# Weight loads on the scalar engine's queue, and a plan that counts transferred bytes, in an attention and channel-mix kernel

## The chip, the cores and the metric

The kernel runs on one core of one Trainium2 chip. The metric is the device time of one execution in microseconds (us), median of three runs. The engines are called by their profile names: PE (matrix products), DVE (VectorE), ACT (ScalarE), POOL (GpSimd) and SP (SyncE, which computes nothing and here issues transfers). Each engine works through its own queue strictly in the order in which the program lists its instructions.

## The reference

Inputs: q, k, v of shape 8 x 8 x 1152 x 64 (batch, heads, tokens, head size) in float32, and the weights of a channel mix, `w_k` 512 x 1024, `w_v` 1024 x 512 and `w_r` 512 x 512. Cut to what matters, the reference computes

```python
q_pool = q.reshape(B, H, S // 2, 2, D).mean(axis=3)          # 576 queries per head
scores = (q_pool @ k.T) / sqrt(D)
attn   = exp(scores - max); attn /= sum(attn) + 1e-9
out    = attn @ v                                            # then heads side by side: x, 8 x 576 x 512
x_prev = x shifted by one token
k = relu((mu_k * x + (1 - mu_k) * x_prev) @ w_k)
r = sigmoid((mu_r * x + (1 - mu_r) * x_prev) @ w_r)
result = r * ((k * k) @ w_v)
```

## The kernel before

**Attention.** A head is loaded by `prep` (keys `kr`, values `vr`, 288 KB each, split there into a coarse and a fine half-precision part `kn`, `vt`, `vb`) and every second head `queries` loads the queries `qr` of two heads in two pieces. Transposing transfers issued by SP (L432, L407) turn `kn` into `ks1` and the queries `qn` into `qT`; L435 copies `ks1` into a second tile `ks2`, which the second pass of scores reads (the trace calls both `ks`). A head has six blocks of 96 queries (`block`), 384 blocks in all. For each block PE makes scores (L473) in one of three buffers `s`, DVE takes the maximum over the keys (`mx`, L480, then `mb`, L486), PE spreads it (L483, L488), ACT writes it beside the fine part of the queries (L491), PE adds the fine part of the scores (L497), ACT exponentiates into `pf` (L503), POOL splits off the low bits `pl` (L505), and `window` multiplies by the values (L523, L525, L530).

**Channel mix.** When the eight heads of a batch element are done, `ff` runs its products (L663) over tiles of 256 tokens. In the first batch element there is no such work yet.

**Weights.** `weights` loads the three matrices in twenty pieces of 512 KB, eight of `w_k`, four of `w_r`, eight of `w_v`, each into one of two staging buffers `st` (L581). A piece is converted by ACT (L592, into the one PSUM bank `f`), three DVE instructions (L594, L595, L597), ACT (L599) and POOL (L600). A buffer of `st` is free again when the L597 of its piece has ended. All twenty conversions lie in the first batch element.

**Order.** No instruction is issued where it is written. The calls of `op` (`Issue.add`) collect 'operations' with an engine, an assumed duration, the buffers read and written, and a key. `Issue.run` then simulates list scheduling under two sets of paddings (`PLANS`), improves the order for eight rounds, judges each order on three trials with randomly lengthened durations and waits, and issues the best one. Each engine's order is thereafter fixed. A transfer is an operation on a planned engine "DMA" (SP's queue): an assumed issue time, then a fixed `tail` until its data are there (2.0 to 4.5 us), whatever else is being transferred; in the trials up to `LATE_DMA` = 1.5 us are added to it. Some buffers are named as read by the first two weight loads only so that the plan puts these loads after them.

**Completion.** Transfers signal through eight semaphores that are used in rotation in the order of the program, and a transfer first waits until the one eight before it has landed.

Of the kernel before, what the change touches and what calls it, by code (L numbers as in the profile page):

```python
# [20 lines left out]
P = 128  # L21
# [20 lines left out]
PER, PACE = 2.75, 2.4  # L42
# [5 lines left out]


PLANS = ((0.08, 0.1), (0.12, 0.15))  # L50
LATE, SLACK, LATE_DMA = 0.06, 0.06, 1.5

class Issue:
# [17 lines left out]
                return self.LAT[k]  # L73
        return 0.18

    def add(self, eng, dur, fn, r=(), w=(), key=0.0, port=None, tail=2.0):
        n = len(self.ops)
        deps = {}

        def dep(m, war):  # L80
            e = self.ops[m][0]
            lat = self.ops[m][6] if e == "DMA" else 0.0 if war and e == eng else self.lat(e, eng)
            deps[m] = max(deps.get(m, 0.0), lat)

# [12 lines left out]
        for b in r:
            if b not in w:
                self.rd.setdefault(b, []).append(n)
        self.ops.append((eng, dur, fn, key, deps, eng == "POOL" if port is None else port, tail))  # L100

    @staticmethod
    def play(eng, dur, pred, succ, prio, wait, port):
# [155 lines left out]
def kernel(  # L259
# [12 lines left out]
    nc = tc.nc  # L272
    B, H, S, D = q.shape
# [16 lines left out]
    const = ctx.enter_context(tc.tile_pool(name="const", bufs=1))  # L290
    psum = ctx.enter_context(tc.tile_pool(name="psum", bufs=1, space=PSUM))
    iss = Issue()
    op = iss.add

    def bufs(name, n, shape, dt):
        return [const.tile(shape, dt, name=f"{name}{i}") for i in range(n)]
# [81 lines left out]
    def queries(n, key):  # L378
# [4 lines left out]
        JS = ((0, 5), (5, NQ))  # L383
        for j0, j1 in JS:
            js = slice(j0, j1)
            op("DMA", 0.36, lambda js=js: nc.sync.dma_start(qr[0][:, js], qv[:, js]), w=[("qr", j0)],
               key=key - 2 * NB * PER, tail=3.0)
            op("DVE", (j1 - j0) * D / 960 + 0.069, lambda js=js: nc.vector.tensor_tensor(
                qs[0][:, js], qr[0][:, js, 0:D], qr[0][:, js, D:2 * D], op=ALU.add),
               r=[("qr", j0)], w=[("qs", j0)], key=key, port=True)  # L390
            op("ACT", (j1 - j0) * P / 1200 + 0.093, lambda js=js, j1=j1, j0=j0: nc.scalar.activation(
                qn[0][:, 0, js].rearrange("p j (r d) -> p j r d", r=2),
                qs[0][:, js].unsqueeze(2).broadcast_to([P, j1 - j0, 2, D]), AF.Copy, scale=SQ),
               r=[("qs", j0)], w=[("qn", j0)], key=key + 1)
            op("DVE", (j1 - j0) * D / 960 + 0.069, lambda js=js: nc.vector.scalar_tensor_tensor(
                qn[0][:, 1, js, 0:D], qs[0][:, js], SQ, qn[0][:, 0, js, 0:D], op0=ALU.mult, op1=ALU.subtract),
               r=[("qs", j0), ("qn", j0)], w=[("qnl", j0)], key=key + 2, port=True)
            if n and j0 == 0:
                continue

            g0 = 0 if n else j0
            gs = slice(g0, j1)
            blocks = [(hh, jj, g) for g, g1 in JS for hh in (0, 1) for jj in range(NB)
                      if g0 <= g < j1 and hh * TQ + jj * QN < g1 * P and hh * TQ + (jj + 1) * QN > g * P]
            js_ = [g for g, _ in JS if g0 <= g < j1]
            for r_, m, t_ in ((0, "qn", "qT"), (1, "qnl", "qTl")):
                op("DMA", 1.25, lambda gs=gs, r_=r_: nc.sync.dma_start_transpose(  # L407
                    qT[i][:, r_, gs], qn[0][:, r_, gs].rearrange("p j x -> p (j x)")),
                   r=[(m, g) for g in js_] + ([("qn", g) for g in js_] if r_ else []),
                   w=[(t_, i) + b_ for b_ in blocks], key=key + 2, tail=2.0)  # L410

    def prep(n, key):

        b, h = divmod(n, H)
        i, j = n % 2, n % NV
        def dma(o, src, buf):
            op("DMA", 0.36, lambda: nc.sync.dma_start(o, src), w=[buf], key=key - 2 * NB * PER, tail=2.8)

        dma(kr[i], k[b, h].rearrange("(p c) d -> p c d", c=NC), ("kr", i))
        dma(vr[i], v[b, h].rearrange("(p c) d -> p c d", c=NC), ("vr", i))  # L420
        for c0, c1 in ((0, 5), (5, NC)):
# [7 lines left out]
               lambda cs=cs, en=nc.vector if ve else nc.gpsimd: en.tensor_tensor(  # L429
                   kn[i][:, cs, D:P], kr[i][:, cs], kn[i][:, cs, 0:D], op=ALU.subtract),  # L430
               r=[("kr", i), ("kn", i, c0)], w=[("knl", i, c0)], key=key + 1, port=True)
        op("DMA", 1.3, lambda: nc.sync.dma_start_transpose(ks1[i], kn[i].rearrange("p c x -> p (c x)")),  # L432
           r=[(m, i, c0) for m in ("kn", "knl") for c0 in (0, 5)], w=[("ks1", i, 0), ("ks1", i, 5)],
           key=key + 1, tail=2.0)
        op("DMA", 0.47, lambda: nc.sync.dma_start(ks2[i][0:D], ks1[i][0:D]),  # L435
           r=[("ks1", i, 0), ("ks1", i, 5)], w=[("ks2", i)], key=key + 1, tail=2.5)
        for c0, c1 in ((0, 5), (5, NC)):
            cs = slice(c0, c1)
            nn = (c1 - c0) * D
# [128 lines left out]
    def weights(n, w, kc, key, step):  # L568
        cols = w.shape[1]
        wv = w.bitcast(I32).rearrange("(c p) (f t) -> c p f t", p=P, t=2)  # L570
        for c in range(kc):
            for f in range(0, cols, 512):
# [8 lines left out]
                op("DMA", 0.36, lambda s3=s3, src=wv[c, :, f:f + 512]: nc.sync.dma_start(s3, src),  # L581
                   r=[("ks1", 1, 0), ("ks2", 0), ("vr", 1)] if iss.nw <= 2 else [], w=[ks], key=key, tail=4.5)
# [64 lines left out]
    def ff(t0, t1, key, tail):  # L647
# [49 lines left out]
        for s0 in range(0, n, P):  # L697
# [24 lines left out]
            for f in range(NF):  # L722
# [4 lines left out]
            op("DVE", 0.605, lambda e=e, m_=m_, ps=ps[:, 0:DM]: nc.vector.scalar_tensor_tensor(  # L727
                m_, ps, 0.5 / (SV * SV * SW), e, op0=ALU.mult, op1=ALU.mult),
               r=[pk, ke], w=[km], key=key + O_DONE)
            op("DMA", 0.36, lambda m_=m_, t=t0 + s0: nc.sync.dma_start(out_f[t:t + P], m_), r=[km], key=key)  # L730
        return key


# [65 lines left out]
```

## Time and profile before

| what | value |
|---|---|
| median of 3 runs | 1170.27 us (1168.08 to 1170.37) |
| the profiled execution's own time | 1168.73 us |
| its span, first to last instruction | 1166.8 us |
| mean granted clock of PE | 0.995 |
| first product of PE | 11.99 us |
| first and last conversion of a weight piece (start of L592) | 27.9 and 147.0 us |

The profile is of one execution, and times in it count from the first instruction. 'Busy' of an engine is the time in which at least one of its instructions ran; the idle time before an instruction is put down to what ended it last. Rows of SP are the times that its queue took to issue a transfer; when the data are there is given apart, as 'to landing'.

### The profile page before, as it was taken

How to read it: one execution, taken by the hardware profiler on the slowest of the kernel's cores; microseconds unless marked ns; L12 is line 12 of the kernel's file. 1: busy time of each engine (PE TensorE's matmuls, PEld its weight loads, DVE VectorE, ACT ScalarE, POOL GpSimd, SP SyncE). 2: the span in 40 equal slices, each digit the busy share in tenths (PEclk: the TensorE clock that was granted, in tenths of full speed). 3: DMA queues.
4: the chain of work that ended last, by engine and by line, in shares of the span. 5: the costliest groups of instructions: out<-in, count | busy, mean ns of one | idle time of the engine just before them, and what ended most of it. 6: DMA issues, size and time to landing. Idle time of an engine off the chain costs nothing.

```text
span 1166.8 us, 45860 instructions
## 1 busy us (share of the span) xinstructions
PE 1116.0 (96%) x19504; PEld 928.6 (80%) x19504; DVE 834.0 (71%) x1558; ACT 858.8 (74%) x1746; POOL 713.1 (61%) x819
## 2 busy tenths in 40 slices
PE   3878899999999999999999999999999999999998
PEld 3767787988788887978788888979797988888565
DVE  6899987777777867777676867776677877673320
ACT  4878887887877787777777686868777778765643
POOL 3777776656666575746666575756665666543431
PEclk9899999999999999999999999999999999999999
DMA  9696845566455534555344535444544344310000
GB/s 223 180 240 171 188 101 129 120 142 113 88 116 117 136 68 103 123 113 123 87 113 114 105 89 119 113 102 108 113 114 107 93 102 93 72 27 12 19 19 28
DMA packets 222380, 126.69 MB, mean 109 GB/s; under 512 B 157664, under 2 KB 194528, under 8 KB 222176
## 3 DMA queue, kind: packets, MB, share of 16 engines
q1 hardware_dynamic: 222176, 123.77, 47.1%
q8 instruction: 152, 2.49, 0.9%
q14 instruction: 52, 0.43, 0.1%
HBM read 67.11 MB, written 9.44 MB: 66 GB/s over the span
## 4 chain that ended last, share of the span: by engine, by line
PE 84%; ACT 5%; DVE 5%; DMA 3%; issue 2%; SPq 0%; ACTq 0%; DVEq 0%
PE f L663 33%; PE s L497 11%; PE s L473 11%; PE a L530 7%; PE a L523 6%; PE a L525 6%; PE s L663 4%; ACT pf L503 2%; DVE mx L480 2%; PE s L483 2%; PE a L663 2%; PE s L488 1%; PE a L560 1%; DMA qT<-qn 1%; DMA st<-in_moe_w_r_dram 1%
## 5 line engine op out<-in xcount | busy, mean ns | idle before, releaser
L505 POOL TENSOR_SCALAR pl<-pf 128x864 f16<-128x864 uint16 x384 | 365.8, 953 | 252.0 <-ACT pf L503 221.2
L480 DVE TENSOR_REDUCE mx<-s 128x96 f16<-128x864 f32 x384 | 402.3, 1054 | 139.1 <-PE s L473 82.1
L503 ACT ACTIVATE pf<-s 128x864 int32<-128x864 f32 x384 | 338.6, 891 | 87.9 <-PE s L497 66.8
L473 PE MATMUL s<-qT,ks 128*128 128x96 f16 x3456 | 217.9, 207 | 23.6 <-DMA qT<-qn 12.0
L525 PE MATMUL a<-vt,pf 128*128 128x64 f16 x2880 | 237.6, 193 | 0.0
L523 PE MATMUL a<-vt,pf 128*128 128x65 f16 x2880 | 237.2, 193 | 0.2
L497 PE MATMUL s<-qT,ks 128*128 128x96 f16 x3456 | 216.0, 207 | 9.7 <-ACT qT L491 8.8
L473 PEld LDWEIGHTS <-ks 128*128 128x128 f16 x3456 | 183.2, 99 | 45.1 <-issue 18.2
L523 PEld LDWEIGHTS <-pf 128*128 128x128 f16 x2880 | 202.3, 98 | 5.6
L497 PEld LDWEIGHTS <-ks 128*128 128x128 f16 x3456 | 181.2, 98 | 31.2 <-issue 12.1
L525 PEld LDWEIGHTS <-pf 128*128 128x128 f16 x2880 | 193.1, 98 | 7.4 <-issue 0.4
L491 ACT ACTIVATE qT<-s 1x96 f16<-1x96 f32 x384 | 92.9, 243 | 111.2 <-PE s L488 97.5
L486 DVE TENSOR_REDUCE mb<-s 96x1 f16<-96x128 f32 x384 | 109.0, 285 | 82.0 <-PE s L483 72.4
L530 PE MATMUL a<-vb,pl 128*128 128x65 f16 x2880 | 152.7, 194 | 1.0 <-POOL pl L505 0.9
L663 PE MATMUL f<-xhk,wk_hi 128*128 128x256 f16 x496 | 135.1, 272 | 0.4 <-ACT r L690 0.4
L663 PE MATMUL f<-xhk,wk_lo 128*128 128x256 f16 x496 | 135.1, 272 | 0.0
L663 PE MATMUL f<-xlk,wk_hi 128*128 128x256 f16 x496 | 135.1, 272 | 0.0
L530 PEld LDWEIGHTS <-pl 128*128 128x128 f16 x2880 | 121.4, 98 | 6.3 <-POOL pl L505 1.6
L663 PEld LDWEIGHTS <-wk_hi 128*128 128x128 f16 x1152 | 106.2, 98 | 10.9 <-issue 0.6
L429 POOL TENSOR_TENSOR kn<-kr,kn 128x320 f16<-128x320 f32 x126 | 99.7, 802 | 20.5 <-ACT kn L424 16.1
L694 POOL TENSOR_TENSOR gl<-g 128x512 f16<-128x512 f32 x72 | 77.8, 1080 | 50.0 <-ACT g L692 47.8
L663 PE MATMUL f<-wv_hi,g 128*128 128x512 f16 x240 | 90.9, 379 | 0.9 <-ACT em L713 0.6
(93 smaller groups left out, 1989.9 us busy)
## 6 DMA issues: line engine op xcount, KB each, us to landing
kr<-in_k_dram SPq DMA_DIRECT2D x64, 288.0 KB, 3.0
vr<-in_v_dram SPq DMA_DIRECT2D x64, 288.0 KB, 3.0
qr<-in_q_dram SPq DMA_DIRECT2D x32, 320.0 KB, 3.5
ks<-ks SPq DMA_DIRECT2D x64, 144.0 KB, 2.6
out_dram<-em SPq DMA_DIRECT2D x36, 256.0 KB, 2.1
qr<-in_q_dram SPq DMA_DIRECT2D x32, 256.0 KB, 3.5
st<-in_moe_w_k_dram SPq DMA_DIRECT2D x8, 512.0 KB, 4.5
st<-in_moe_w_v_dram SPq DMA_DIRECT2D x8, 512.0 KB, 4.0
```

What stands on the lines that cost most here:

```text
L429: lambda cs=cs, en=nc.vector if ve else nc.gpsimd: en.tensor_tensor(kn[i][:, cs, D:P], kr[i][:, cs], kn[i][:, cs, 0:D], op=ALU.subtract),
L473: nc.tensor.matmul(cols(c, c + 1), ks1[hp][:, c, :], qhi, start=(c == c0), stop=False, skip_group_check=True)
L480: op("DVE", 0.967, lambda: nc.vector.tensor_reduce(mxz, grid(0, NC).rearrange("p c q -> p q c"), axis=AX.X, op=ALU.max), r=[("s", z)], w=[ ...
L486: op("DVE", 0.199, lambda: nc.vector.tensor_reduce(mbz[0:QN], s[0:QN, 0:P], axis=AX.X, op=ALU.max), r=[("s", z)], w=[("mb", z)], key=t + O ...
L491: op("ACT", 0.133, lambda: nc.scalar.activation(qlo[QN:QN + 1], s[QN:QN + 1, 0:QN], AF.Prelu, scale=1.0 - EPS, alpha=(1.0 + EPS) / (1.0 - ...
L497: nc.tensor.matmul(cols(c, c + 1), ks2[hp][:, c, :], qlo, start=False, stop=True, skip_group_check=True)
L503: op("ACT", NC * QN / 1200 + 0.051, lambda: nc.scalar.activation(pf[:, :, rows], grid(0, NC), AF.Exp, bias=SHIFT, scale=0.125 / (2.0 * SQ) ...
L505: op("POOL", NC * QN / 1000 + 0.066, lambda: nc.gpsimd.tensor_scalar(pl[:, :, rows], half(pf, U16, 0)[:, :, rows], LO, 1.0, op0=ALU.mult, ...
L523: nc.tensor.matmul(a_b[:, a0:a0 + VN], half(pf, F16, 1)[:, c, rows], vt[jv][:, c, D:D + VN], start=(w == 0 and c == 0), stop=False, skip_g ...
L525: nc.tensor.matmul(a_b[:, a0:a0 + D], half(pf, F16, 1)[:, c, rows], vt[jv][:, c, 0:D], start=False, stop=False, skip_group_check=True)
L530: nc.tensor.matmul(a_b[:, a0:a0 + VN], pl[:, c, rows], vb[jv][:, c, 0:VN], start=False, stop=(c == NC - 1), skip_group_check=True)
L663: nc.tensor.matmul(ps, terms[i][0], terms[i][1], start=(first and i == 0), stop=(i == last), skip_group_check=True)
```

## The change

It has four parts.

- A new method `move` enters a transfer as two planned operations: its issue on the engine that issues it, and, `lead` = 1.0 us later, its bytes on a planned resource "BYTES" that serves one transfer at a time at 215 KB per us, with 0.4 us until the data count as there. All transfers but the two small ones of `mu_k` and `mu_r` use it. "BYTES" issues nothing; it exists in the plan alone.
- The twenty weight loads are issued by ACT (`nc.scalar.dma_start`), with an assumed issue time of 0.40 us, and their key is lower by two steps of the sequence of pieces.
- `LATE_DMA` is 0.8 in place of 1.5.
- The fixed tails go, since `move` replaces them.

```diff
-LATE, SLACK, LATE_DMA = 0.06, 0.06, 1.5
+LATE, SLACK, LATE_DMA = 0.06, 0.06, 0.8
...
-            lat = self.ops[m][6] if e == "DMA" else 0.0 if war and e == eng else self.lat(e, eng)
+            lat = self.ops[m][6] if self.ops[m][6] else 0.0 if war and e == eng else self.lat(e, eng)
...
+    def move(self, kb, eng, dur, fn, r=(), w=(), key=0.0, lead=1.0, tail=0.4):
+
+        self.add(eng, dur, fn, r=r, w=w, key=key, tail=lead)
+        self.add("BYTES", kb / 215.0, lambda: None, r=r, w=w, key=key, tail=tail)
...
-            op("DMA", 0.36, lambda: nc.sync.dma_start(o, src), w=[buf], key=key - 2 * NB * PER, tail=2.8)
+            move(288, "DMA", 0.4, lambda: nc.sync.dma_start(o, src), w=[buf], key=key - 2 * NB * PER)
...
-        op("DMA", 0.47, lambda: nc.sync.dma_start(ks2[i][0:D], ks1[i][0:D]),
-           r=[("ks1", i, 0), ("ks1", i, 5)], w=[("ks2", i)], key=key + 1, tail=2.5)
+        move(200, "DMA", 0.47, lambda: nc.sync.dma_start(ks2[i][0:D], ks1[i][0:D]),
+           r=[("ks1", i, 0), ("ks1", i, 5)], w=[("ks2", i)], key=key + 1)
...
-                op("DMA", 0.36, lambda s3=s3, src=wv[c, :, f:f + 512]: nc.sync.dma_start(s3, src),
-                   r=[("ks1", 1, 0), ("ks2", 0), ("vr", 1)] if iss.nw <= 2 else [], w=[ks], key=key, tail=4.5)
+
+                move(512, "ACT", 0.40, lambda s3=s3, src=wv[c, :, f:f + 512]: nc.scalar.dma_start(s3, src),
+                   r=[("ks1", 1, 0), ("ks2", 0), ("vr", 1)] if iss.nw <= 2 else [], w=[ks], key=key - 2.0 * step)
```

The same instructions with the same operands are issued as before, apart from the queue of the twenty loads. But the plan is made anew, so the order changes on every engine. In the new file the lines lie 6 or 7 further down: L581 is L588, L592 is L599, L597 is L604, L480 is L486, L486 is L492, L491 is L497, L503 is L509, L407 is L413, L417 is L423, L432 is L438, L435 is L441. Numbers behind a name tell its buffers apart (`ks_0_79` and `ks_1_80` are the two `ks1`, `ks_0_81` and `ks_1_82` the two `ks2`; `st_121` and `st_120` the two staging buffers).

Three places matter below. The first is the start: SP's queue behind the first eight loads (keys, values, queries and the two `mu`). Before:

```order
L432 DMA_TRANSPOSE ks_0_79<-kn_76 128x9x128
L386 DMA qr_74<-in_q_dram 128x5x128
L407 DMA_TRANSPOSE qT_83<-qn_78 128x5x128
L386 DMA qr_74<-in_q_dram 128x4x128
L435 DMA ks_0_81<-ks_0_79 64x1152
```

Now:

```order
L392 DMA qr_74<-in_q_dram 128x5x128
L413 DMA_TRANSPOSE qT_83<-qn_78 128x5x128 x2
L438 DMA_TRANSPOSE ks_0_79<-kn_76 128x9x128
L438 DMA_TRANSPOSE ks_1_80<-kn_77 128x9x128
L392 DMA qr_74<-in_q_dram 128x4x128
L413 DMA_TRANSPOSE qT_83<-qn_78 128x4x128 x2
L441 DMA ks_0_81<-ks_0_79 64x1152
```

The first queries are turned ahead of the first keys, and the copy into the first `ks2` has moved behind four further transposing transfers.

The second is where the weight loads begin. SP's queue before (a few us after the rows above):

```order
L417 DMA kr_70<-in_k_dram 128x576
L407 DMA_TRANSPOSE qT_83<-qn_78 128x4x128
L581 DMA st_121<-in_moe_w_k_dram 128x1024
L581 DMA st_120<-in_moe_w_k_dram 128x1024
L435 DMA ks_1_82<-ks_1_80 64x1152
L417 DMA vr_72<-in_v_dram 128x576
L386 DMA qr_74<-in_q_dram 128x5x128
L386 DMA qr_74<-in_q_dram 128x4x128
```

ACT's queue before, behind the second exponential (`kr_70` and `vr_72` hold the third head's keys and values here):

```order
L491 ACTIVATE qT_83<-s_130 1x96
L391 ACTIVATE qn_78<-qs_75 128x512
L424 CAST kn_76<-kr_70 128x5x64
L424 CAST kn_76<-kr_70 128x4x64
L503 ACTIVATE pf<-s_130 128x9x96
L440 ACTIVATE vt_87<-vr_72 128x5x64
L592 ACTIVATE f<-st_121 128x512
L491 ACTIVATE qT_83<-s_128 1x96
```

ACT's queue now, from the first block's L491 (now L497) to the first conversion:

```order
L497 ACTIVATE qT_83<-s_128 1x96
L588 DMA st_121<-in_moe_w_k_dram 128x1024
L588 DMA st_120<-in_moe_w_k_dram 128x1024
L497 ACTIVATE qT_83<-s_129 1x96
L509 ACTIVATE pf<-s_128 128x9x96
L397 ACTIVATE qn_78<-qs_75 128x512
L509 ACTIVATE pf<-s_129 128x9x96
L497 ACTIVATE qT_83<-s_130 1x96
L430 CAST kn_76<-kr_70 128x5x64
L430 CAST kn_76<-kr_70 128x4x64
L509 ACTIVATE pf<-s_130 128x9x96
L599 ACTIVATE f<-st_121 128x512
```

The two loads have left SP's queue, and `vt_87`, which reads the third head's values, no longer stands ahead of the first conversion; it comes five rows after the last one shown, behind the fifth exponential.

The third is the end of the conversions, in DVE's queue. Before, the twentieth stands ahead of the maximum of the 57th block:

```order
L595 SCALAR_TENSOR_TENSOR f<-st_120,f 128x512
L486 TENSOR_REDUCE mb_97<-s_129 96x1
L597 SCALAR_TENSOR_TENSOR ex_116<-st_120,f 128x512
L480 TENSOR_REDUCE mx_95<-s_130 128x96
L545 TENSOR_SCALAR den_99<-a 128x5
```

Now it stands ahead of that of the 52nd:

```order
L492 TENSOR_REDUCE mb_98<-s_130 96x1
L602 SCALAR_TENSOR_TENSOR f<-st_120,f 128x512
L604 SCALAR_TENSOR_TENSOR ex_116<-st_120,f 128x512
L486 TENSOR_REDUCE mx_93<-s_128 128x96
L449 SCALAR_TENSOR_TENSOR vt_87<-vr_72,vt_87 128x4x64
```

So the conversions end five blocks earlier. In PE's queue the first product of the channel mix moves with them, from behind the scores of 57 blocks to behind those of 52.

More of the change, by code (lines that the diff above doesn't have):

```diff
@@ L74, in lat, with add @@
         return 0.18
-    def add(self, eng, dur, fn, r=(), w=(), key=0.0, port=None, tail=2.0):
+    def add(self, eng, dur, fn, r=(), w=(), key=0.0, port=None, tail=None):
         n = len(self.ops)
@@ L99, in add @@
                 self.rd.setdefault(b, []).append(n)
-        self.ops.append((eng, dur, fn, key, deps, eng == "POOL" if port is None else port, tail))
+        self.ops.append((eng, dur, fn, key, deps, eng == "POOL" if port is None else port,
+                         2.0 if eng == "DMA" and not tail else tail))
+    def move(self, kb, eng, dur, fn, r=(), w=(), key=0.0, lead=1.0, tail=0.4):
+        self.add(eng, dur, fn, r=r, w=w, key=key, tail=lead)
+        self.add("BYTES", kb / 215.0, lambda: None, r=r, w=w, key=key, tail=tail)
     @staticmethod
@@ L292 @@
     iss = Issue()
-    op = iss.add
+    op, move = iss.add, iss.move
     def bufs(name, n, shape, dt):
@@ L385, in queries @@
             js = slice(j0, j1)
-            op("DMA", 0.36, lambda js=js: nc.sync.dma_start(qr[0][:, js], qv[:, js]), w=[("qr", j0)],
-               key=key - 2 * NB * PER, tail=3.0)
+            move((j1 - j0) * 64, "DMA", 0.5, lambda js=js: nc.sync.dma_start(qr[0][:, js], qv[:, js]), w=[("qr", j0)],
+               key=key - 2 * NB * PER)
             op("DVE", (j1 - j0) * D / 960 + 0.069, lambda js=js: nc.vector.tensor_tensor(
@@ L406, in queries @@
             for r_, m, t_ in ((0, "qn", "qT"), (1, "qnl", "qTl")):
-                op("DMA", 1.25, lambda gs=gs, r_=r_: nc.sync.dma_start_transpose(
+                move(110, "DMA", 1.25, lambda gs=gs, r_=r_: nc.sync.dma_start_transpose(
                     qT[i][:, r_, gs], qn[0][:, r_, gs].rearrange("p j x -> p (j x)")),
                    r=[(m, g) for g in js_] + ([("qn", g) for g in js_] if r_ else []),
-                   w=[(t_, i) + b_ for b_ in blocks], key=key + 2, tail=2.0)
+                   w=[(t_, i) + b_ for b_ in blocks], key=key + 2)
     def prep(n, key):
@@ L431, in prep @@
                r=[("kr", i), ("kn", i, c0)], w=[("knl", i, c0)], key=key + 1, port=True)
-        op("DMA", 1.3, lambda: nc.sync.dma_start_transpose(ks1[i], kn[i].rearrange("p c x -> p (c x)")),
+        move(110, "DMA", 1.3, lambda: nc.sync.dma_start_transpose(ks1[i], kn[i].rearrange("p c x -> p (c x)")),
            r=[(m, i, c0) for m in ("kn", "knl") for c0 in (0, 5)], w=[("ks1", i, 0), ("ks1", i, 5)],
-           key=key + 1, tail=2.0)
-        op("DMA", 0.47, lambda: nc.sync.dma_start(ks2[i][0:D], ks1[i][0:D]),
-           r=[("ks1", i, 0), ("ks1", i, 5)], w=[("ks2", i)], key=key + 1, tail=2.5)
+           key=key + 1)
+        move(200, "DMA", 0.47, lambda: nc.sync.dma_start(ks2[i][0:D], ks1[i][0:D]),
+           r=[("ks1", i, 0), ("ks1", i, 5)], w=[("ks2", i)], key=key + 1)
         for c0, c1 in ((0, 5), (5, NC)):
@@ L729, in ff @@
                r=[pk, ke], w=[km], key=key + O_DONE)
-            op("DMA", 0.36, lambda m_=m_, t=t0 + s0: nc.sync.dma_start(out_f[t:t + P], m_), r=[km], key=key)
+            move(256, "DMA", 0.36, lambda m_=m_, t=t0 + s0: nc.sync.dma_start(out_f[t:t + P], m_), r=[km], key=key)
         return key
```

## Prediction

> **What bounds the kernel now.** I read the page first (busy shares), then the stretches, then the timeline of the stretch that stood out.
>
> ```profile
> span 1166.8 us, 45860 instructions
> PE 1116.0 (96%) x19504; PEld 928.6 (80%) x19504; DVE 834.0 (71%) x1558; ACT 858.8 (74%) x1746; POOL 713.1 (61%) x819
> ```
>
> PE bounds the whole, but 1166.8 - 1116.0 = 50.8 us of its span are idle. The view of stretches tells where; its columns are the busy time of each engine, PE's clock, the share in which the transfer engines are busy, and GB/s.
>
> ```profile
> core 0: us, PE busy (x) PEld busy (x) DVE busy (x) ACT busy (x) POOL busy (x), PEclk, DMA share, GB/s
> 13.00:37.00 24.00, 16.65 (x239) 15.22 (x237) 13.45 (x24) 12.44 (x25) 9.84 (x12) 0.79 0.98 226
> 37.00:146.00 109.00, 88.19 (x1956) 78.33 (x1957) 106.28 (x200) 89.55 (x180) 82.18 (x91) 1.00 0.81 192
> 146.00:233.00 87.00, 84.44 (x1470) 71.93 (x1468) 67.55 (x125) 69.16 (x142) 60.83 (x67) 1.00 0.54 117
> 233.00:1050.00 817.00, 812.79 (x14826) 687.27 (x14824) 605.78 (x1127) 625.09 (x1275) 516.64 (x593) 1.00 0.47 104
> 1050.00:1167.00 117.00, 112.90 (x1013) 74.71 (x1011) 31.92 (x61) 56.91 (x116) 38.65 (x47) 0.99 0.05 19
> ```
>
> After 146 us PE idles 2.6 + 4.2 + 4.1 = 10.9 us in 1021: nothing to win there. From 37 to 146 us, while the weights are converted, DVE is busy 106.28 of 109 us and PE waits for it: that stretch is as long as DVE's list. From 13 to 37 us no engine is full: DVE idles 10.55 of 24 us, and the transfers are busy 0.98 of the time. Since DVE bounds what follows, an idle us of DVE here is a us of the kernel. The timeline names these (start, duration, in brackets the idle time before and what ended it):
>
> ```profile
> 15.91 0.24 ACT L491 ACTIVATE qT<-s 1x96 f16<-1x96 f32 x1 [1.66 <-PE s L488]
> 17.61 1.04 SPq L581 DMA_DIRECT2D st<-in_moe_w_k_dram  x2
> 19.33 0.69 SPq L417 DMA_DIRECT2D vr<-in_v_dram  x1
> 20.99 0.89 ACT L503 ACTIVATE pf<-s 128x864 int32<-128x864 f32 x1
> ...
> 27.50 0.47 ACT L440 ACTIVATE vt<-vr 128x320 f16<-128x320 f32 x1 [5.62 <-DMA vr<-in_v_dram]
> 27.87 0.61 ACT L592 ACTIVATE f<-st 128x512 f32<-128x512 f32 x1
> 28.51 0.70 DVE L594 TENSOR_SCALAR f<-f 128x512 int32<-128x512 int32 x1 [4.34 <-ACT f L592]
> 30.42 0.29 DVE L486 TENSOR_REDUCE mb<-s 96x1 f16<-96x128 f32 x1 [0.48 <-PE s L483]
> 32.91 1.06 DVE L480 TENSOR_REDUCE mx<-s 128x96 f16<-128x864 f32 x1 [1.60 <-ACT pf L503]
> 34.69 1.06 DVE L480 TENSOR_REDUCE mx<-s 128x96 f16<-128x864 f32 x1 [0.72 <-ACT f L592]
> 36.59 0.29 DVE L486 TENSOR_REDUCE mb<-s 96x1 f16<-96x128 f32 x1 [0.84 <-PE s L483]
> ```
>
> The reader is to see one chain. Two weight loads of 512 KB go out at 17.61 on the one queue; the third head's values go out behind them at 19.33 and are there at 27.50, 8.2 us later. ACT, strictly in order, stands 5.62 us at L440; the first conversion, the exponentials and the next L491 stand behind it; DVE stands 4.34 us, and while ACT catches up four times more.
>
> **The stall goes.** In the new order of ACT, `vt` of these values stands behind the fifth exponential, the loads of the values go out two rows after the second copy `ks2`, and the weight loads have another queue. What is late next is the first conversion, which needs its own load. The two loads go out behind the first L491, which ran at 15.91 before, say at 16.9 with the delay found below. ACT comes to the conversion after three L491, three L503, one L391 and two casts; the same rows had ended at 20.99 + 0.89 = 21.9 before, so with that delay (0.7) and the two issues (1.04 on SP) near 23.6 us. How long such loads take:
>
> ```profile
> L581 SPq DMA_DIRECT2D st<-in_moe_w_k_dram x8: 328/526/1387, 17.6 to 64.5; - x8
> L581 SPq DMA_DIRECT2D st<-in_moe_w_v_dram x8: 328/346/455, 97.8 to 139.4; - x8
> L581 SPq DMA_DIRECT2D st<-in_moe_w_r_dram x4: 328/328/478, 68.3 to 92.1; - x4
> DMA to landing us min/median/max: 3.5/4.3/6.8
> ```
>
> 16.9 + 4.3 to 6.8 is 21.2 to 23.7, so the conversion hardly waits. The second piece is wanted near 28; by then 1024 KB of weights, two heads' keys and one's values (864 KB) and 576 KB of queries must have passed, 2.5 MB, at the 226 GB/s of the stretch 11.1 us from 16.9: 28.0. So all five gaps go: 4.34 + 0.48 + 1.60 + 0.72 + 0.84 = 8.0 us. Bounds: 8.0, or 1.8 if only the lesser four shrink by half and the rest returns as another wait.
>
> A rule speaks against the change. The Trainium skill, page "DMA: Bandwidth & Descriptors", section "Issuing engines are not separate DMA queues", says that transfers issued by different engines run on the same 16 transfer engines and interleave, so that a second queue saves only the time to issue. The 0.98 above agrees that these engines, not the queue, were full. By the rule alone the gain is nothing, and it is a rival below; I take the 8.0, since it comes from the new order of the readers and not from bytes that travel faster.
>
> **The start is later.** Rows of the start, and the copy's time to landing from the page:
>
> ```profile
> 5.64 2.07 SPq L432 DMA_TRANSPOSE ks<-kn  x1
> 8.42 1.21 SPq L407 DMA_TRANSPOSE qT<-qn  x1
> 10.36 0.54 SPq L435 DMA_DIRECT2D ks<-ks  x1
> 11.99 2.32 PE L473 MATMUL s<-qT,ks 128*128 128x96 f16 x27 [11.99 <-DMA qT<-qn]
> 16.21 0.88 PE L497 MATMUL s<-qT,ks 128*128 128x96 f16 x9 [0.33 <-ACT qT L491]
> ks<-ks SPq DMA_DIRECT2D x64, 144.0 KB, 2.6
> ```
>
> The first product needs one transposing transfer of queries and one of keys. Before, the keys' went first; now two of queries go ahead, and the first product waits for the keys. One more transfer of 1.21 us in the row, partly within waits that were there: 0.5 us. The copy into `ks2` was there at about 10.36 + 2.6 = 13.0, 3.2 us before its reader at 16.21. Now four more transposing transfers stand ahead of it (4 x 1.21 = 4.8 us): it lands at 17.8 at the latest, earlier if they fill waits that were there, and the reader is ready at 16.7. Together +0.7 us, nearer the low end, since SP also waited between these rows before; bounds 0 and 2.0.
>
> **Conversions come earlier on DVE.** In the new order all 20 lie ahead of the 52nd block's L480, where before 18 did. DVE's rows from 37 to 146 us:
>
> ```profile
> L480 DVE TENSOR_REDUCE mx<-s 128x96 f16<-128x864 f32 x46 | 47.6, 1047 | 1.9 <-PE s L488 0.6 <-PE s L473 0.6 <-issue 0.2
> L594 DVE TENSOR_SCALAR f<-f 128x512 int32<-128x512 int32 x18 | 12.3, 686 | 0.3 <-ACT f L592 0.3
> L595 DVE SCALAR_TENSOR_TENSOR f<-st,f 128x512 int32<-128x512 int32 x18 | 12.3, 681 | 0.0
> L597 DVE SCALAR_TENSOR_TENSOR ex<-st,f 128x512 int32<-128x512 int32 x18 | 12.2, 677 | 0.3
> L443 DVE SCALAR_TENSOR_TENSOR vt<-vr,vt 128x320 f16<-128x320 f32 (+1 forms) x14 | 7.8, 571 | 0.0
> 1140.00 0.27 PE L663 MATMUL s<-xhk,wk_hi 128*128 128x256 f16 x1
> 1140.11 0.27 PE L663 MATMUL s<-xlk,wk_hi 128*128 128x256 f16 x1
> ```
>
> A conversion takes (12.3 + 12.3 + 12.2) / 18 = 2.04 us of DVE; two more are 4.1, less one L443 that has moved behind (0.57): 3.5 us later at that block. But PE has done more by then, eight products of the channel mix at the 0.11 us between the last two rows (0.9) and a few of the values (0.2): net +2.4 us, up to where PE, with products to do, no longer waits for DVE. Bounds: 0 (if PE has spare work there) and 4.1.
>
> **ACT issues twenty loads.** By SP's medians that is 8 x 0.526 + 8 x 0.346 + 4 x 0.328 = 8.3 us, 18 of the 20 (7.5 us) from 37 to 146 us. ACT idles 109 - 89.55 = 19.45 us there, DVE 2.72. The loads lie beside DVE's work, except where DVE waits for ACT; if DVE's idle time grows as ACT's shrinks (19.45 / 11.95), it becomes 4.4: +1.7 us. No trace shows a load issued by ACT. Bounds: -2.7, since SP is freed of loads that wait for `st`, and DVE's remaining gaps could go with that; and +7.5, every issue on the path. I take +1.7, near the low end, as ACT stays the emptier engine. Behind a waiting load stand ACT's L491 and L503, and DVE behind those; but most loads stand next to an L592 that waits for the same L597, since both `f` and `st` come free with it. A load may also wait for the signal of a transfer of SP's eight places before; in the order these went out long enough before, so nothing is set for it.
>
> What lies past 146 us is ordered anew from the same lists; DVE's and ACT's last 40 rows are the same, so I put 0 there, 2 us either way.
>
> **Sum.** -8.0 + 0.7 + 2.4 + 1.7 = -3.2 us, on the profiled execution's 1168.73: 1165.5. That execution lies 1.54 below the median of the runs, so against the median: 1170.27 - 3.2 = 1167.1 us.
>
> **Rivals.** *More.* ACT's issue costs nothing and SP's freed queue closes DVE's last gaps: -8.0 + 0.7 + 2.4 - 2.7 = -7.6, 1162.7 us. For it: DVE needs no more than its list. Against it: ACT's list is longer.
>
> *Nothing.* The bytes due by 37 us are the same and the transfers were full (0.98), so the wait returns at a conversion or at the next head's values: -1.8 + 0.7 + 2.4 = +1.3, and ACT's part between -2.7 and +1.7: 1168.9 to 1173.3, the middle 1171.1 us.
>
> *ACT waits out SP's issues.* If two queues share what makes transfers ready, a load on ACT stands until SP's transposing transfer is through.
>
> ```profile
> L432 SPq DMA_TRANSPOSE ks<-kn x9: 1297/1725/2417, 29.0 to 144.0; - x9
> L407 SPq DMA_TRANSPOSE qT<-qn x9: 1201/1629/5149, 16.4 to 132.8; - x9
> ```
>
> From 17 to 146 us these take 9 x 1.73 + 9 x 1.63 = 30.2 of 129 us, 23%; half of one is 0.85, so 0.2 us for each load, 3.6 for 18: ACT's idle falls to 8.35, DVE's rises to 6.3, +3.6 in place of +1.7: 1169.0 us. The Trainium skill, page "Perfetto Trace Analysis", section "DMA Instruction — HWDGE (DVE, Sync)", states such a lock on a shared descriptor generator; by it this rival is the case, and no run here shows it yet.
>
> *Slower: the two staging buffers become the pace.* A load starts when the conversion two before has ended and must land before the next one has. From 37 to 146 us DVE does 106.28 - 36.8 = 69.5 us beside conversions, for 46 blocks, 1.51 each. From the first to the last conversion were 50 blocks, (50 x 1.51 + 19 x 2.04) / 19 = 6.0 us apart; now 45, 5.6 apart. Landing takes 4.3 us at the median, so 1.3 us are spare, but 6.8 at worst, and now loads share the transfer engines with SP's queue instead of following it in turn. It decides from a median of 5.6 on. At 6.8, 18 loads are 1.2 us late, 21.6 us of ACT; DVE bridges most with the three `s` buffers, and a third coming through is +7.2: 1167.1 + 7.2 = 1174.3 us.
>
> **Numbers.** 0.2% of 1170 is 2.3 us, about what a measurement here tells from no change: faster is below 1167.9, slower above 1172.6. The forecast 0.43 (own range 1164 to 1169.5: 0.33 faster, 0.10 same); more 0.14 (faster); nothing 0.11 (0.02, 0.06, 0.03 slower); waiting out SP 0.11 (0.02, 0.08, 0.01); staging buffers 0.21 (0.02 same, 0.19 slower). Faster 0.51, same 0.26, slower 0.23. The range of 8 in 10 goes from the upper half of 'more' to the staging buffers' price, 1161.5 to 1174.3.
>
> **What would show it.** Right: no gap of ACT over 1 us ahead of `vt<-vr` and none of DVE over 1 us from 22 to 37 us; the first conversion near 23.6 us instead of 27.9; the seventh maximum ended near 29 instead of 34; the first L497 (now L503) near 17; DVE idle 3 to 5 us from 30 to 140. Wrong: ACT idle ahead of L599 by DMA `st`, or weight loads that land in over 5.6 us at the median (staging buffers); issue rows of ACT over 1 us beside SP's transposing ones (waiting out); a gap of 4 us or more before 40 us (nothing).

## The result and the profile after

The changed kernel took 1163.98 us (median of 8 executions, 1162.04 to 1166.12) beside 1170.23 us of the kernel before on the same chip: ratio 0.9949, 95% interval 0.9937 to 0.9961, 6.2 us faster. The forecast was 1167.1, 3.2 us faster, in a range of 1161.5 to 1174.3. Two further lots of the same order, run for the experiments below, gave 0.9965 (0.9952 to 0.9979) and 0.9960 (0.9946 to 0.9973), so the gain is 4 to 6 us, and its middle nearer 5. The profiled execution took 1164.98 us, 3.75 less than the one before; it lies 1.0 us above the median of its kernel and the one before 1.5 below, so this pair shows less than the medians do.

The page and the stretches of after, in the columns of those shown of before:

```profile
span 1163.2 us, 45837 instructions
PE 1116.5 (96%) x19504; PEld 932.3 (80%) x19504; DVE 837.8 (72%) x1558; ACT 858.4 (74%) x1746; POOL 706.8 (61%) x819
```

```profile
13.00:37.00 24.00, 19.62 (x362) 17.58 (x362) 19.19 (x36) 16.77 (x34) 13.56 (x16) 1.00 1.06 243
37.00:146.00 109.00, 86.69 (x1770) 78.83 (x1769) 97.88 (x186) 84.11 (x166) 77.20 (x84) 0.89 0.79 182
146.00:233.00 87.00, 86.37 (x1544) 74.53 (x1542) 73.50 (x130) 71.29 (x147) 61.97 (x71) 1.00 0.59 132
233.00:1050.00 817.00, 814.49 (x14889) 689.89 (x14887) 609.52 (x1130) 626.47 (x1282) 512.15 (x592) 1.00 0.46 103
1050.00:1167.00 117.00, 109.30 (x953) 71.51 (x949) 29.33 (x55) 54.39 (x109) 37.33 (x45) 0.99 0.05 19
```

From 13 to 37 us DVE does 19.19 us of work in place of 13.45: the stall is gone. From 37 to 146 us it does 8.4 us less than before, PE's clock was granted at 0.89 in place of 1.00, and DVE, which had been full, idles 11.1 us in place of 2.7. From 233 to 1050 us PE idles 2.5 us in place of 4.2. So a lead is won early and lost again, and something is won late.

Rows picked from the timeline of after, at the start and at the place of the old stall (L497, L599, L601, L486 and L492 are the old L491, L592, L594, L480 and L486):

```profile
13.05 2.34 PE L479 MATMUL s<-qT,ks 128*128 128x96 f16 x27 [13.05 <-DMA ks<-kn]
16.57 1.07 ACTq L588 DMA_DIRECT2D st<-in_moe_w_k_dram  x2
18.05 0.90 PE L503 MATMUL s<-qT,ks 128*128 128x96 f16 x9 [1.53 <-DMA ks<-ks]
24.07 0.63 ACT L599 ACTIVATE f<-st 128x512 f32<-128x512 f32 x1
24.74 0.70 DVE L601 TENSOR_SCALAR f<-f 128x512 int32<-128x512 int32 x1
27.39 0.78 ACT L446 ACTIVATE vt<-vr 128x320 f16<-128x320 f32 x2
27.70 2.01 DVE L486 TENSOR_REDUCE mx<-s 128x96 f16<-128x864 f32 x2
30.32 0.29 DVE L492 TENSOR_REDUCE mb<-s 96x1 f16<-96x128 f32 x1 [0.60 <-PE s L489]
```

The values' `vt` is ready without a wait, the first conversion starts at 24.07, and the pair of maxima at 27.70 (the seventh and the eighth) has ended at 29.7; the eighth ended at 35.7 before. But the first L503 is at 18.05, 1.84 us later than its L497 was.

How to measure the lead beyond that? PE does the same 19504 products in every kernel here, so I count its **lag**: the time, less the steady cost of all products begun by then (each at the ns that it takes back to back in the trace of before; 1089.9 us in all; other choices of that cost, from 1076 to 1100 us in all, move no difference in the table by over 0.1 us). Two kernels with the same lag have done the same share of PE's work. A rise in lag is time that PE lost. Lag in us, of one execution each:

| at us | before | after | after minus before |
|---|---|---|---|
| 37 | 27.45 | 23.20 | -4.25 |
| 75 | 39.14 | 36.65 | -2.49 |
| 95 | 45.90 | 47.93 | +2.03 |
| 146 | 62.45 | 65.17 | +2.72 |
| 233 | 66.24 | 66.02 | -0.22 |
| 400 | 66.88 | 66.74 | -0.14 |
| 700 | 72.05 | 69.01 | -3.04 |
| 1150 | 72.89 | 69.22 | -3.67 |

I call what is lost up to 233 us, while weights are converted and shortly after, the head, and the rest the body. No weight load lies in the body: the last goes out at 132.1 us. In this pair of executions the head gained nothing, and the body gained 6.65 - 3.20 = 3.45 us, where the forecast had 0.

### The profile page after: what moved, and what is told of

It is laid out like the page before. It is cut to its first block, busy times and chain, and to the rows that moved or that the text cites. A ratio compares the mean times of both kernels' runs of the same rounds, so it can differ in the third digit from the quotient of the medians.

```text
span 1163.2 us, 45837 instructions
## 1 busy us (share of the span) xinstructions
PE 1116.5 (96%) x19504; PEld 932.3 (80%) x19504; DVE 837.8 (72%) x1558; ACT 858.4 (74%) x1746; POOL 706.8 (61%) x819
## 3 DMA queue, kind: packets, MB, share of 16 engines
q8 instruction: 152, 2.49, 0.9%
## 4 chain that ended last, share of the span: by engine, by line
PE 87%; ACT 4%; DMA 3%; DVE 3%; issue 2%; SPq 0%; POOL 0%; ACTq 0%; DVEq 0%
PE f L670 34%; PE s L503 11%; PE s L479 11%; PE a L536 7%; PE a L529 7%; PE a L531 7%; PE s L670 4%; PE s L489 2%; PE a L670 2%; ACT pf L509 2%; PE a L566 1%; PE s L494 1%; DVE mx L486 1%; DMA ks<-kn 1%; DMA qT<-qn 1%
## 5 line engine op out<-in xcount | busy, mean ns | idle before, releaser
L486 DVE TENSOR_REDUCE mx<-s 128x96 f16<-128x864 f32 x384 | 402.4, 1054 | 132.6 <-PE s L479 84.9
L509 ACT ACTIVATE pf<-s 128x864 int32<-128x864 f32 x384 | 338.6, 890 | 89.3 <-PE s L503 65.5
L503 PE MATMUL s<-qT,ks 128*128 128x96 f16 x3456 | 216.3, 208 | 9.8 <-ACT qT L497 7.5
L503 PEld LDWEIGHTS <-ks 128*128 128x128 f16 x3456 | 181.8, 99 | 30.5 <-issue 9.8
L531 PEld LDWEIGHTS <-pf 128*128 128x128 f16 x2880 | 193.8, 98 | 10.2 <-issue 1.3
L497 ACT ACTIVATE qT<-s 1x96 f16<-1x96 f32 x384 | 92.8, 243 | 105.8 <-PE s L494 96.7
L492 DVE TENSOR_REDUCE mb<-s 96x1 f16<-96x128 f32 x384 | 109.7, 286 | 84.2 <-PE s L489 75.7
L435 POOL TENSOR_TENSOR kn<-kr,kn 128x320 f16<-128x320 f32 x126 | 97.7, 783 | 24.7 <-ACT kn L430 20.1
L489 PE MATMUL s<-identb,mx 128*96 128x128 f16 x384 | 87.5, 228 | 5.8 <-DVE mx L486 5.5
```

Source lines behind the costliest of these rows:

```text
L486: op("DVE", 0.967, lambda: nc.vector.tensor_reduce(mxz, grid(0, NC).rearrange("p c q -> p q c"), axis=AX.X, op=ALU.max), r=[("s", z)], w=[ ...
L489: op("PE", 0.054, lambda: nc.tensor.matmul(s[0:QN, 0:P], mxz, identb, start=False, stop=False, skip_group_check=True), r=[("mx", z)], w=[( ...
L492: op("DVE", 0.199, lambda: nc.vector.tensor_reduce(mbz[0:QN], s[0:QN, 0:P], axis=AX.X, op=ALU.max), r=[("s", z)], w=[("mb", z)], key=t + O ...
L503: nc.tensor.matmul(cols(c, c + 1), ks2[hp][:, c, :], qlo, start=False, stop=True, skip_group_check=True)
L509: op("ACT", NC * QN / 1200 + 0.051, lambda: nc.scalar.activation(pf[:, :, rows], grid(0, NC), AF.Exp, bias=SHIFT, scale=0.125 / (2.0 * SQ) ...
L531: nc.tensor.matmul(a_b[:, a0:a0 + D], half(pf, F16, 1)[:, c, rows], vt[jv][:, c, 0:D], start=False, stop=False, skip_group_check=True)
```

## The experiments

**1. Which part gains?** Two kernels in which both plans are computed; the operations up to the first product of the 100th block are issued in the order of one plan, all others in that of the other (`HEAD` is "new" in the first kernel and "old" in the second).

```diff
+HEAD, CUT = "new", 100
...
+        for u in head[:cut]:
+            self.fns[u][z]()
+        for u in tail:
+            if u not in first:
+                self.fns[u][1 - z]()
```

> The order of the changed kernel up to the first product of the 100th block of scores (about 233 us), with the weight loads on ACT; from there the order of the kernel before. Theory A (the gain comes from the stretch that holds the weight loads, since no operation waits behind them on SP any more): 1164 us, like the changed kernel, with PE's lag behind its steady work at 1050 us about 3 us under that of before. Theory B (the gain comes from the newly planned order past 233 us, where the traces of before and after part): 1169 to 1171 us, like before, since the head's lead is given back between 37 and 146 us (PE's lag at 233 us was 66.2 before and 66.0 after). If each holds half: 1167 us.

> The reverse: the order of before up to the 100th block of scores, with the weight loads on SP, and from there the order of the changed kernel. Theory A: 1170 us, like before, with the 4.34 us gap of ACT at 26 us. Theory B: 1165 to 1167 us, the gap at 26 us still there and the small stalls of PE from 400 to 700 us gone.

(The 4.34 us at 26 us named there are DVE's gap; ACT stood 5.62 us.)

New head and old rest: 1167.59 us beside 1169.76, ratio 0.9988 (0.9968 to 1.0008). Old head and new rest: 1167.91, ratio 0.9991 (0.9980 to 1.0003). Neither has the gain of the whole, and neither alone can be told from no change. The lags say more. From 233 us to 1150 the old body lost 6.65 us in before and 71.81 - 64.94 = 6.87 behind the new head. The new body lost 3.20 in after and 70.51 - 65.37 = 5.14 behind the old head, of which 2.5 us fell between 233 and 300 us, where the two orders meet (after lost 0.66 there), so in that kernel the body's gain is 1.5 us and not 3.45. Away from the seam the body's loss repeats. From 400 to 700 us, rows of before and of the new head with the old rest, then of after and of the old head with the new rest:

```profile
400.00:700.00 300.00, 297.26 (x5372) 251.39 (x5370) 218.82 (x407) 229.96 (x468) 192.97 (x224) 1.00 0.48 105
```

```profile
400.00:700.00 300.00, 297.29 (x5356) 251.11 (x5353) 219.14 (x409) 229.08 (x467) 192.47 (x223) 1.00 0.49 106
```

```profile
400.00:700.00 300.00, 298.61 (x5391) 252.32 (x5387) 226.09 (x411) 229.68 (x470) 192.60 (x223) 1.00 0.47 108
```

```profile
400.00:700.00 300.00, 298.61 (x5397) 252.41 (x5394) 226.28 (x409) 230.72 (x471) 194.04 (x224) 1.00 0.48 108
```

The same body idles PE by 2.7 us or by 1.4 us there, whichever head stood in front. The loss consists of small waits: from 233 us on PE stood for over 0.25 us beyond its steady pace 15 times in before (6.3 us in all) and 10 times in after (3.8 us), mostly for an `xt`, `em`, `qT` or `pf` of ACT that came late. One of them in before:

```profile
409.91 0.54 PE L473 MATMUL s<-qT,ks 128*128 128x96 f16 x9 [0.68 <-ACT pf L503]
```

**2. The queue alone.** Each order with the loads on the other queue, and nothing planned anew. The new order:

```diff
-                move(512, "ACT", 0.40, lambda s3=s3, src=wv[c, :, f:f + 512]: nc.scalar.dma_start(s3, src),
+                move(512, "ACT", 0.40, lambda s3=s3, src=wv[c, :, f:f + 512]: nc.sync.dma_start(s3, src),
```

The old order:

```diff
-                op("DMA", 0.36, lambda s3=s3, src=wv[c, :, f:f + 512]: nc.sync.dma_start(s3, src),
+                op("DMA", 0.36, lambda s3=s3, src=wv[c, :, f:f + 512]: nc.scalar.dma_start(s3, src),
```

> The changed kernel's order with one edit: the weight loads are issued by SP at their places in that order. If the queue matters (heads' transfers stand behind loads that wait for a staging buffer): 1170 us or more, with gaps of ACT or DVE between 22 and 37 us. If the order alone matters: 1162 to 1166 us, and a gap under 1 us there. By theory B: 1164 us, as past 233 us it is the changed kernel's.

> The kernel before with one edit: the weight loads are issued by ACT at their places in the old order. If the queue matters: the gap of 4.34 us at 26 us shrinks below 1 us and the time is 1165 to 1168 us. If the plan matters: the loads stand late in ACT's list, the gap shrinks but the staging buffers' loads wait behind ACT's other work, 1169 to 1172 us. By theory B: 1170 us, the lead of the head being lost by 146 us.

New order with loads on SP: 1166.44, ratio 0.9973 (0.9960 to 0.9986); ACT stood 2.76 us at 27 us and 1.92 us at 38 us for DMA `st`, and the body lost 3.33 us, as expected of the new one. So the new order alone keeps over half of the gain, and whether the second queue adds to it (0.9949, 0.9965 and 0.9960 in the three lots) isn't clear of the noise. Old order with loads on ACT: 1173.81, ratio 1.0035 (1.0022 to 1.0048), slower by 4.05 us. I had expected 1165 to 1172. Between 37 and 75 us its lag went from 1.1 us under that of before to about 3.5 over, and one landing stands out there; queue and engine rows of one stretch, then the stretch:

```profile
55.92 2.29 SPq L432 DMA_TRANSPOSE ks<-kn  x1
59.60 6.34 SPq L407 DMA_TRANSPOSE qT<-qn  x1
...
57.21 0.34 ACTq L581 DMA_DIRECT2D st<-in_moe_w_k_dram  x1
...
66.56 0.76 ACT L424 CAST kn<-kr 128x320 f16<-128x320 f32 x2 [5.26 <-DMA ks<-kn]
...
69.18 0.29 DVE L486 TENSOR_REDUCE mb<-s 96x1 f16<-96x128 f32 x1 [6.36 <-PE s L483]
```

```profile
60.00:66.50 6.50, 1.19 (x33) 1.08 (x31) 2.82 (x6) 0.78 (x2) 2.32 (x3) 0.87 1.14 122
```

The keys' transposing transfer goes out at 55.92 and a weight load follows on the other queue 1.3 us later, which on SP had to wait for its turn. The transfer lands 10.6 us after its issue, where the same one in before took 4.4. ACT's next cast may not overwrite `kn` until then and stands 5.26 us, and with it DVE (6.36) and PE (1.19 us of work in 6.5). The transfer engines were full (1.14) all the while. So here the other queue added no room: it let 512 KB in between. That this one landing is all of the 4 us is not shown.

Do such landings slow the changed kernel too? Transposing transfers of keys from 17 to 146 us, time to landing in us, in before, in after, in the second profile of the changed kernel (below), and in the new order with the loads on SP:

```profile
L432 SPq DMA_TRANSPOSE ks<-kn x9: 1297/1725/2417, 29.0 to 144.0; - x9
DMA to landing us min/median/max: 3.2/4.1/4.7
```

```profile
L438 SPq DMA_TRANSPOSE ks<-kn x8: 1379/2128/2426, 28.4 to 133.5; - x8
DMA to landing us min/median/max: 4.3/5.6/7.5
```

```profile
L438 SPq DMA_TRANSPOSE ks<-kn x8: 1293/1941/2407, 27.0 to 136.0; - x8
DMA to landing us min/median/max: 3.5/5.2/10.2
```

```profile
L438 SPq DMA_TRANSPOSE ks<-kn x8: 1256/1680/2347, 27.7 to 138.4; - x8
DMA to landing us min/median/max: 3.2/5.1/5.9
```

The median is 1.0 to 1.5 us above before in all three profiles of the new order, on either queue, and 3.6 us in the next order of the planner with the loads on ACT (experiment 6), so it comes with the order. The latest landing was longer on ACT's queue (7.5 and 10.2 us, and 10.9 in the third profile below) than with the same order on SP (5.9); but with the loads on ACT it was 5.9 and 5.5 too, in the new head with the old rest and in experiment 4, so this isn't told from chance. The Trainium skill, page "DMA: Bandwidth & Descriptors", section "Issuing engines are not separate DMA queues", says that such transfers interleave on the same 16 engines; the landing of 10.6 us beside 4.4 agrees in direction.

In after, though, no engine waited for a transfer of keys from 37 to 146 us, and with the loads on SP the same order lost as much there: its lag rose by about 42.6 us (after 42.0, before 35.0). Its stretch, in the columns above, and what DVE waited for in after (us in total, times, longest):

```profile
37.00:146.00 109.00, 87.38 (x1772) 79.75 (x1771) 96.89 (x183) 84.59 (x166) 76.16 (x84) 0.86 0.75 183
```

```profile
DVE mb L492 <- PE s L489: 6.5, 8, 1.7
DVE mx L486 <- PE s L479: 2.7, 5, 1.2
```

So this profile speaks against the second queue as what loses the early lead. All seven profiles with this order in that stretch have PE's clock at 0.84 to 0.89 there, before at 1.00, which is taken up at the end.

**3. How much is one execution's chance?** The changed kernel again, and the changed kernel with other random numbers in the planner's trials.

```diff
-        trials = [times(LATE, SLACK, 1 + i) for i in range(3)]
+        trials = [times(LATE, SLACK, 11 + i) for i in range(3)]
```

> The changed kernel once more, for a second profile. Theory AB (head and body both): 1162 to 1166 us; lead over before in PE's lag about 4 us at 37 us, 0 to 2 at 233 us, and 3 more gained from 400 to 700 us (2.3 us of lag there, as in every kernel with the new body so far, against 5.1 to 5.6 with the old). If the gain of the body is chance of a single execution: 3 to 6 us of lag there.

> The changed kernel with one edit: the three noisy trials by which its planner picks one of its orders use other random numbers, so another order may be picked. Theory 'the rules of the new plan' (bytes as a resource order the body better): 1162 to 1166 us, and 2 to 3 us of PE's lag from 400 to 700 us. Theory 'the draw' (the body's gain is a matter of which order came out): another lag there, anywhere from 2 to 6 us, and a time between 1162 and 1170 us. If the same order is picked, the time is the changed kernel's.

The other numbers picked the same order, so that run is a third profile of the changed kernel, and tells nothing of rules against draw. The three executions took 1164.98, 1166.49 and 1168.76 us. Their lags at 233 us are 66.02, 67.43 and 69.79; their bodies lost 3.20, 3.30 and 3.10. The body repeats within 0.2 us and the head varies by 3.8. A single pair of profiles therefore says little of the head; for that the times must speak.

**4. The later start.** In the new order the first keys' transposing transfer is moved ahead of the second one of the queries, and the copy into the first `ks2` up by two transposing transfers and a load.

```diff
+        for a, b in ((("qT", 0, 0, 1), ("kT", 0)), (("kC", 0), ("kT", 1))):
+            order.remove(tag[a])
+            order.insert(order.index(tag[b]) + 1, tag[a])
```

> The changed kernel's order with two DMA moves of SP's first ones: the transposing transfer of the first head's keys goes ahead of the second one of the queries, and its copy to the second set of keys goes right behind the next head's keys, four transfers earlier. If the later start (+1.8 us at the first product with the second set, forecast +0.7) is paid for in full: that product near 16.3 us in place of 18.05, and 1.5 to 1.9 us less in the end, 1162.2 us. If the lead is lost between 37 and 146 us whatever it was: 1164 us, and the lag at 146 us as in the changed kernel (65.2).

(The copy goes out three transfers earlier, not four.)

The product stood at 15.55 in place of 18.05, more than expected, and the time was 1166.42, ratio 0.9970 (0.9959 to 0.9980): nothing gained on the changed kernel.

```profile
15.26 1.20 ACTq L594 DMA_DIRECT2D st<-in_moe_w_k_dram  x2
15.55 0.88 PE L509 MATMUL s<-qT,ks 128*128 128x96 f16 x9 [0.33 <-ACT qT L503]
16.85 0.58 SPq L429 DMA_DIRECT2D kr<-in_k_dram  x1
23.57 0.77 ACT L436 CAST kn<-kr 128x320 f16<-128x320 f32 x2 [4.28 <-DMA kr<-in_k_dram]
```

The weight loads went out 1.3 us sooner with the product, so that 1024 KB went out ahead of the third head's keys, issued at 16.85, and ACT waited 4.28 us for these keys. 2.5 us won at the start were lost by 25 us (lag 20.59 beside 19.80 to 20.63).

**5. The staging buffers.** The rival that forecast them as the pace had one sign: ACT stood once for a weight piece in after, ahead of the row at 78.66. It stood twice in the second profile (up to 3.02 us) and three times in the third (4.80 us ahead of 39.53, then 0.86 and 2.09).

```profile
78.66 0.63 ACT L599 ACTIVATE f<-st 128x512 f32<-128x512 f32 x1 [2.79 <-DMA st<-in_moe_w_r_dram]
```

```diff
-    st = bufs("st", 2, [P, 1024], I32)
+    st = bufs("st", 3, [P, 1024], I32)
...
+        for k in range(20, 3, -1):
+            order.remove(tag["st", k])
+            order.insert(order.index(tag["st", k - 1]) + 1, tag["st", k])
```

> The changed kernel's order with a third staging buffer, each weight load from the fourth on issued by ACT at the place where the load before it stood, so a whole conversion earlier. If the loss from 37 to 146 us is that of two staging buffers (ACT's 2.79 us gap at 78.66 us, DMA st, and PE's half clock behind it): no gap of ACT by DMA st over 0.5 us, fewer slices at half clock, lag at 146 us 62 to 63 in place of 65.2, and 1 to 3 us less in the end. If the loss is that DVE holds more conversions in that stretch: the lag at 146 us stays within 1 us of 65.2, half clock as before, 1163 to 1165 us.

1166.25 us, ratio 0.9964 (0.9948 to 0.9980), as the changed kernel in the same lots (0.9960 and 0.9965). Lag at 146 us 65.88, within 1 us of 65.17 and below the 66.27 and 67.15 of the other two executions. One gap by DMA `st` remained, 2.24 us at 36.45. So the staging buffers are not what the lead is lost to. PE's clock stayed at 0.87 from 37 to 146 us, so this run doesn't tell what a full clock would be worth.

**6. Bytes, queue, or just another order?** Setting `LATE_DMA` to 0.8 in the old plan leaves every row of every order as it was, so it needed no run. Three kernels instead: the second best of each planner's own orders, and the changed kernel with its transfers planned as before (no "BYTES"), the loads still on ACT.

```diff
-                if best is None or total < best[0]:
-                    best = (total, order)
+                if order not in [o for _, o in seen]:
+                    seen.append((total, order))
...
+        seen.sort(key=lambda x: x[0])
+        best = seen[1]
```

```diff
-        self.add(eng, dur, fn, r=r, w=w, key=key, tail=lead)
-        self.add("BYTES", kb / 215.0, lambda: None, r=r, w=w, key=key, tail=tail)
+        self.add(eng, dur, fn, r=r, w=w, key=key, tail=4.5 if eng == "ACT" else 2.4)
```

> The changed kernel with the second best of its planner's own orders in place of the best: same rules, another order in the body too. PE's lag gained from 233 us to the end was 6.65 to 6.87 us in the three kernels with the old order of the body and 3.1 to 3.3 in the four with the new one. Theory 'rules' (counting bytes orders the body better): 2.5 to 4 us here, 1163 to 1168 us. Theory 'draw' (which order comes out is chance, under either plan): anything from 2 to 8 us, and as likely over 5 as under.

> The kernel before with the second best of its planner's own orders. Theory 'rules': 6 to 7.5 us of lag from 233 us to the end, 1169 to 1172 us. Theory 'draw': anything from 2 to 8 us, 1164 to 1172 us.

> The changed kernel without the bytes as a resource in its plan: a transfer again holds only its queue, and lands 2.4 us later (4.5 for a weight load), as in the plan before; the weight loads stay on ACT. Theory 'rules': the body's lag goes back to 6 to 7 us, and the head is worse as well since the loads are not spaced: 1168 to 1172 us. Theory 'draw': a body's lag from 2 to 8 us that has nothing to do with the bytes.

And the fourth place of that square, bytes counted and the loads planned for and issued by SP:

```diff
-                move(512, "ACT", 0.40, lambda s3=s3, src=wv[c, :, f:f + 512]: nc.scalar.dma_start(s3, src),
+                move(512, "DMA", 0.40, lambda s3=s3, src=wv[c, :, f:f + 512]: nc.sync.dma_start(s3, src),
```

> The changed kernel with the weight loads planned for SP's queue and issued by it: bytes counted, no load on ACT. It fills the fourth place beside before (SP, no bytes), the changed kernel (ACT, bytes) and the one without bytes (ACT, no bytes; 0.9954). Theory 'queue' (the gain of the head needs the loads off SP): a lag at 233 us of 66 us or more, as before, and 1167 to 1171 us, with a body's lag of its own between 3 and 7 us. Theory 'bytes' (the spaced plan is enough): a lag at 233 us of 64 to 66 us and 1163 to 1166 us.

| loads planned on | bytes counted | time, us | ratio to before (95%) | lag at 233 | lost by the body |
|---|---|---|---|---|---|
| SP (before) | no | 1169.66 | 1 | 66.2 | 6.65 |
| SP, next order | no | 1171.10 | 1.0014 (1.0004 to 1.0024) | 70.8 | 5.8 |
| SP | yes | 1168.83 | 0.9986 (0.9976 to 0.9996) | 68.5 | 4.4 |
| ACT | no | 1163.24 | 0.9954 (0.9940 to 0.9967) | 63.7 | 3.8 |
| ACT (after) | yes | see above | 0.9949, 0.9965, 0.9960 | 66.0 to 69.8 | 3.1 to 3.3 |
| ACT, next order | yes | 1165.29 | 0.9965 (0.9953 to 0.9978) | 64.3 | 4.7 |

Three orders planned with the loads on ACT gain 0.35 to 0.5%; three planned for SP lie between 0.14% faster and 0.14% slower. Counting bytes is worth nothing that shows beside the queue: without it the kernel was as fast (0.9954). I had expected 1168 to 1172 of it, and was wrong. Its stretch and its transposing transfers of keys, in the columns above:

```profile
37.00:146.00 109.00, 91.17 (x1945) 81.62 (x1942) 102.43 (x195) 90.01 (x176) 80.95 (x90) 0.94 0.77 190
```

```profile
L437 SPq DMA_TRANSPOSE ks<-kn x9: 1266/1442/2228, 30.2 to 143.0; - x9
DMA to landing us min/median/max: 3.2/4.2/5.5
```

Those land in 4.2 us, as in before, and DVE idles 6.6 us in place of 11.1. Why the body's order comes out better stays open. The square isn't clean in one point: the two kernels planned by the old rules also keep the old keys of the loads, and the earlier keys were not tried alone. The body's loss varies with the order drawn (5.8 and 6.65 by the same old rules; 3.1 to 3.3 and 4.7 by the same new ones), and the best order on SP (4.4) lies below the worst on ACT (4.7). With no weight load in that stretch, nothing of the queue itself can act there.

## Why the prediction was right, and where it wasn't

The time lay in the range and on the side to which it gave most. By its steps:

- **The stall goes, -8.0.** Right. No gap of ACT ahead of `vt<-vr` before 129 us, none of DVE over 0.60 us from 22 to 37; the first conversion at 24.07 (forecast 23.6); the seventh maximum ended at 28.8 (forecast 29). The eighth ended 6.0 us earlier with a start that was 1.84 us later, so the gaps were worth 7.8.
- **The start, +0.7.** Too small: +1.84 at the first L503 (18.05 in place of "near 17"). The copy landed near 18.0, at what I had called its latest (17.8); I took a value near the low end because SP also waited there before, and the four transfers did not fit into those waits.
- **Conversions and issues, +2.4 and +1.7.** The issue cost is as told: 0.334 us a load at the median, 0.65 at most, so no load waited out a transposing transfer. One of them, at 89.93, fell within a transposing transfer's row of 2.76 us and took 0.33. But DVE was to idle 3 to 5 us from 30 to 140 us, and idled 11.65 (before 6.2): 4.25 us of lead at 37 us were a lag of 2.72 at 146. What failed is the premise that this stretch "is as long as DVE's list", so that an idle us of DVE saved ahead of it is a us of the kernel. In after DVE does 8.4 us less there and idles 11.1, of which 10.1 for products of PE. Why PE is late there stays open. Experiment 2 speaks against the second queue and experiment 5 against the staging buffers, each by one profile; PE's half clock, which comes with this order, is a rival that wasn't tried. In this pair the loss is made up again by 233 us (-0.22).
- **Together the head.** Forecast -3.2. The direct measure is the new head with the old rest, 0.9988: -1.4 us, between -3.7 and +0.9. The whole less the body's 3.45 leaves -0.6 to -2.6. Smaller than forecast is likely, not certain.
- **Past 146 us, 0.** This step failed. "After 146 us PE idles ...: nothing to win there" reads the busy share of PE as if it left nothing. From 233 us on the old body lost 6.65 us of PE's time, most of it in small waits, and the new one 3.1 to 3.3 in every profile: -3.45 us in the first pair, outside the 2 us either way that the prediction allowed. That is over half of the whole.

So the sum was near the truth by luck: a head that gained less than forecast and a body forecast at nothing made up for each other, -1.4 - 3.45 = -4.9, beside the measured -4 to -6. The mechanism that the prediction priced, the stall that goes, is there, but most of the gain came from elsewhere.

Of the rivals, "nothing" had a gap of 4 us or more before 40 us as its sign. It is not in after, but in the third profile ACT stood 4.80 us up to 39.53, so a late transfer does come back in some executions. What this rival missed is the body. "ACT waits out SP's issues" isn't seen. "Staging buffers" had gaps of ACT in all three profiles, but the loads landed in 5.2 us at the median in after, under the 5.6 from which it was to decide, and a third buffer changed nothing that shows.

## What to carry to other kernels

When a change makes a planner order the program anew, forecast the whole of it: an order is drawn again where nothing was edited, and here that was worth over half the gain. Moving transfers to a second queue takes away waits in line but not bytes, and a load that it lets through can make a neighbour land later (10.6 us in place of 4.4 here): look at what is in flight where the large loads go out. Compare two kernels by the work that their bounding engine has done at a given time, over several executions: it shows which stretch repeats and which varies.

## What the runs showed that I had not expected

In these traces PE's clock changes in whole steps of 3.41 us, and PE need not be idle for a whole step to lose it. Rows of after, with PE's busy time, its clock, the DMA share and GB/s:

```profile
43.90:47.30 3.40, 2.43 (x57) 1.00 0.75 219
47.30:50.70 3.40, 1.76 (x26) 1.00 0.59 192
50.70:54.10 3.40, 2.79 (x30) 0.50 0.69 185
54.10:57.50 3.40, 3.35 (x37) 0.50 1.06 197
57.50:60.90 3.40, 3.40 (x108) 1.00 0.81 234
```

PE was busy 1.76 of 3.4 us, and the next window ran at half; after one that was full the clock came back. Over the fourteen profiles here the clock fell about 50 times, after windows in which PE was busy for 0 to 71%; it stayed full after windows of 48% and more, and came back after 82% and more. So the busy share of one window doesn't settle it. The Trainium skill, page "TensorE: Matmul & The Clock Gate", section "What's actually happening", gives a free-running window of 3413 ns, which agrees with the 3.41 us, and an idle window as the condition for the half clock; here windows half busy sufficed. After ran 24 us of its stretch from 37 to 146 us at half clock and before none (before had its half clock in the stall, 10.2 us from 25.7 us), which goes with DVE's longer idle time there (waits for products of PE). Whether the half clock costs time or only follows from waits wasn't tried.
